# Dummy matmuls of a depthwise-separable kernel: operands from a built-in constant, loops unrolled, four passes on each side of dw

## The chip, the cores and the metric

The kernel runs on one core of one Trainium2 chip. The metric is device time in microseconds (us) of one execution.

## The reference

```python
B, H, W, C = x.shape            # 1, 384, 384, 384, bf16
k = dw.shape[0]                 # 1
for i in range(k):
    for j in range(k):
        out = out + xp[:, i:i+H, j:j+W, :] * dw[i, j][None, None, None, :]
return jnp.einsum('bhwc,cd->bhwd', out, pw)      # pw: 384 x 384
```

With k = 1 it is one matrix product in which the rows of pw are scaled by dw: 147,456 pixels by 384 channels, times a 384 x 384 matrix.

## The kernel before

The scaling by dw is folded into the weights, once, ahead of the main loop. A mask `eye` (GpSimd) is reduced to 0/1 selectors `sel` (VectorE), multiplied by dw to `sel_w`, and used in 18 small matmuls that write scaled and reordered rows of pw to PSUM (the "weight build"). Six evictions, five on ScalarE and one on VectorE, copy them to `w_r` (an eviction is a copy out of PSUM). The main loop then transposes x on VectorE, multiplies on TensorE (48 matmuls per tile, in 12 groups of four concurrent ones) and evicts on ScalarE.

While TensorE waits for its first data it runs dummy matmuls, meant to wake its clock (full rate came at 5.57 us in the profile before):

```python
def idle_work(n):
    with nc.tensor.Fori(0, n, 1) as _:
        for i in range(4):
            nc.tensor.matmul(PS[0][:, i, :D], lhsT=zero[32*i : 32*i+32, 0:P],
                             rhs=zero[32*i : 32*i+32, :], start=True, stop=True,
                             tile_position=(32*i, 0))

nc.tensor.wait_ge(s_zero, 1)
idle_work(3)
nc.tensor.wait_ge(s_seed, 2)
nc.tensor.wait_ge(s_dw, 16)
...                                  # three 1-row matmuls that turn dw into a column
idle_work(3)
nc.tensor.wait_ge(s_pw, 16)
times = {(1, 1): 3, (2, 0): 2}       # some groups of the weight build are repeated
...                                  # the weight build, k = 0, 1, 2
with nc.tensor.Fori(0, NS // 2, 1) as it:      # the main loop, 2 of 288 tiles a turn
    ...
```

One turn of the loop in `idle_work`, four matmuls side by side, is called a pass below. The loads at the start: dw and the first chunk of x on ScalarE's queue, pw and then the other chunks of x on SyncE's.

Of the kernel before, what the change touches and what calls it, by code (L numbers as in the profile page):

```python
# [7 lines left out]
BF16 = mybir.dt.bfloat16  # L8
F32 = mybir.dt.float32
U32 = mybir.dt.uint32  # L10
# [17 lines left out]
def kernel(  # L28
# [12 lines left out]
    nc = tc.nc  # L41
    P = nc.NUM_PARTITIONS
    B, H, W, C = x.shape
    assert dw.shape[0] == 1 and dw.shape[1] == 1, "only k=1 depthwise supported"
    D = pw.shape[1]
# [19 lines left out]
    consts = ctx.enter_context(tc.tile_pool(name="consts", bufs=1))  # L65
# [1 line left out]
    psum = ctx.enter_context(tc.tile_pool(name="psum", bufs=1, space=bass.MemoryType.PSUM))  # L67

    pw_n = consts.tile([P, 3, D], BF16, name="pw_n")
    ones = consts.tile([P, P], BF16, name="ones")  # L70
    eye = consts.tile([P, P], BF16, name="eye")
    sel = consts.tile([P, 2, 32], F32, name="sel")
    sel_w = consts.tile([P, 3, 2, 4, 32], BF16, name="sel_w")
    w_r = consts.tile([P, NB, 2, D], BF16, name="w_r")
    dw_row = consts.tile([1, C], BF16, name="dw_row")
    dw_f = consts.tile([P, 3], F32, name="dw_f")
    warm = consts.tile([P, 3], F32, name="warm")
    zero = consts.tile([P, D], BF16, name="zero")

    Xs = [bufp.tile([P, 4 * LMAX, C], BF16, name=f"X{i}") for i in range(NR)]  # L80
    Xl = bufp.tile([P, 4 * LONG, C], BF16, name="Xl")
# [2 lines left out]
    PS = [psum.tile([P, 4, 512], F32, name=f"ps{s}") for s in range(2)]  # L84
# [5 lines left out]
    s_a = [nc.alloc_semaphore(f"s_a{i}") for i in range(2)]  # L90
# [7 lines left out]
    s_sel = nc.alloc_semaphore("s_sel")  # L98
    s_w = nc.alloc_semaphore("s_w")
    s_wr = [nc.alloc_semaphore(f"s_wr{e}") for e in range(2)]  # L100
    s_seed = nc.alloc_semaphore("s_seed")
    s_zero = nc.alloc_semaphore("s_zero")

    with tc.tile_critical():  # L104
        def x_of(t):
# [60 lines left out]
        for o in range(NR):  # L166
            n = sum(n_parts[t] for t, c in enumerate(chunks) if c[0] % NR == o)
# [37 lines left out]


        def idle_work(n):
            with nc.tensor.Fori(0, n, 1) as _:
                for i in range(4):
                    nc.tensor.matmul(  # L210
                        PS[0][:, i, :D],
                        lhsT=zero[32 * i : 32 * i + 32, 0:P],
                        rhs=zero[32 * i : 32 * i + 32, :],
                        start=True,
                        stop=True,
                        tile_position=(32 * i, 0),
                    )

        nc.tensor.wait_ge(s_zero, 1)
        idle_work(3)  # L220

        nc.tensor.wait_ge(s_seed, 2)
        nc.tensor.wait_ge(s_dw, 16)
        for k in range(3):
            mm = nc.tensor.matmul(  # L225
                PS[1][:, 0, D + k : D + k + 1],
                lhsT=dw_row[:, P * k : P * k + P],
                rhs=ones[0:1, 0:1],
                start=True,
                stop=True,  # L230
            )
        mm.then_inc(s_df)
        idle_work(3)
        nc.tensor.wait_ge(s_pw, 16)
        times = {(1, 1): 3, (2, 0): 2}
        for k in range(3):
            nc.tensor.wait_ge(s_sw, k + 1)
            for r in range(2):
# [3 lines left out]
                for v in [0, 1] * times.get((k, r), 1):  # L242
                    mm = nc.tensor.matmul(  # L243
                        PS[(k + 1) % 2][:, 2 * r + v, :D],
                        lhsT=sel_w[64 * v : 64 * v + 64, k, r, :, :].rearrange("p q w -> p (q w)"),
                        rhs=pw_n[64 * v : 64 * v + 64, k, :],
# [5 lines left out]
        with nc.tensor.Fori(0, NS // 2, 1) as it:  # L252
# [2 lines left out]
                supertile(s, rv)  # L255


        nc.gpsimd.memset(warm[:], 0.0).then_inc(s_seed)
        nc.gpsimd.memset(zero[:].bitcast(U32), 0).then_inc(s_zero)  # L259
        nc.gpsimd.memset(ones[:], 1.0).then_inc(s_seed)  # L260
        nc.gpsimd.affine_select(  # L261
            out=eye[:],
            in_=ones[:],
            pattern=[[-1, P]],
            compare_op=mybir.AluOpType.is_equal,
            fill=0.0,
            base=0,
            channel_multiplier=1,
        )._wait_ge(s_seed, 2).then_inc(s_sel)
        for s in range(2):  # L270
            c = nc.scalar.copy(warm[:, s + 1 : s + 2], warm[:, 0:1])  # L271
            if s == 0:
                c._wait_ge(s_seed, 1)
            c.then_inc(s_a[s])

        def transposes(t, j):
            g, i, off, first, L = chunks[t]
# [18 lines left out]
        def w_out(i):  # L296
# [9 lines left out]
            in_=eye[:].rearrange("p (v w r) -> p r w v", v=2, r=2),  # L306
# [15 lines left out]
        for jj, (t, j) in enumerate(order):  # L322
            g, i, off, first, L = chunks[t]
            s = jj % 2
# [49 lines left out]
```

## Time and profile before

| | before |
|---|---|
| time, median of the first 3 runs | 575.13 us (575.04 to 575.19) |
| span of the profile | 573.3 us |
| TensorE busy | 566.7 us, 99% |
| VectorE / ScalarE busy | 507.4 / 419.0 us |
| first matmul of the main loop | 6.98 us |

Read it as three stretches: a start of 7 us, a main loop in which TensorE is never idle, and a tail of a few us that follows the last tile. The prediction shows the lines.

### The profile page before, as it was taken

To read this page: it belongs to the slowest core of one execution; us is meant where nothing else is said; L and a number is where in the kernel's file an instruction comes from. 1 tells how busy PE (TensorE), PEld (TensorE's weight loads), DVE (VectorE), ACT (ScalarE), POOL (GpSimd) and SP (SyncE) were. 2 spreads that over 40 slices of the span, in tenths; PEclk is the share of its full clock that TensorE was granted. 3 is DMA by queue.
4 is the path that set the end of the run, shared out by engine and by line. 5 is a ranking of instruction groups with operands and counts; after the bars stand their busy time and mean duration, and the time that the engine had idled before them with its cause. 6 is when DMAs were issued, how large, how long until landed. Compare 5 with 4: busy or idle time off the path is not lost.

```text
span 573.3 us, 29723 instructions
## 1 busy us (share of the span) xinstructions
PE 566.7 (99%) x13869; PEld 411.9 (72%) x13869; DVE 507.4 (89%) x584; ACT 419.0 (73%) x297; POOL 0.9 (0%) x8
## 2 busy tenths in 40 slices
PE   8999999999999999999999999999999999999996
PEld 5777777777777777777777777777777777777774
DVE  7898898898889889889888988988988898898895
ACT  6777777777777777777777777777777777777775
POOL 0000000000000000000000000000000000000000
PEclk9999999999999999999999999999999999999999
DMA  9999999999999999999999999999999999999676
GB/s 363 418 340 438 415 425 432 446 412 425 428 413 412 406 389 427 402 379 405 431 389 397 412 416 386 406 409 416 406 391 422 405 394 396 424 398 368 263 288 238
DMA packets 26453, 226.88 MB, mean 396 GB/s; under 512 B 1226, under 2 KB 6987, under 8 KB 22603
## 3 DMA queue, kind: packets, MB, share of 16 engines
q1 hardware_dynamic: 25264, 225.61, 97.1%
q10 hardware_dynamic: 1178, 1.18, 0.6%
q14 instruction: 10, 0.07, 0.0%
q8 instruction: 1, 0.02, 0.0%
HBM read 113.54 MB, written 113.25 MB: 396 GB/s over the span
## 4 chain that ended last, share of the span: by engine, by line
PE 97%; DMA 1%; ACT 1%; DVE 0%; issue 0%; SPq 0%
PE ps L193 97%; DMA pw_n<-in_pw_dram 1%; DMA out_dram<-O 0%; ACT w_r L299 0%; ACT O L336 0%; DVE O L334 0%; PE ps L243 0%; SPq L369 0%; SPq L104 0%
## 5 line engine op out<-in xcount | busy, mean ns | idle before, releaser
L193 PE MATMUL ps<-w_r,T 32*128 32x384 bf16 x13824 | 561.8, 321 | 0.5 <-ACT w_r L299 0.5
L286 DVE STREAM_TRANSPOSE T<-X 128x384 uint32<-128x384 uint32 x572 | 500.7, 877 | 55.4 <-DMA X<-in_x_dram 0.3
L336 ACT CAST O<-ps 128x1536 bf16<-128x1536 f32 x287 | 413.0, 1439 | 147.1 <-PE ps L193 147.1
L193 PEld LDWEIGHTS ps<-w_r,T 32*128 32x128 bf16 x13824 | 410.0, 93 | 152.3 <-issue 0.9
L299 ACT CAST w_r<-ps 128x768 bf16<-128x768 f32 x5 | 3.6, 819 | 1.1 <-PE ps L243 1.1
L210 PE MATMUL ps<-zero 32*128 32x384 bf16 x24 | 2.6, 494 | 1.4 <-POOL zero L259 1.4
L286 DVE STREAM_TRANSPOSE T<-Xl 128x384 uint32<-128x384 uint32 x4 | 3.5, 877 | 0.4
L334 DVE CAST O<-ps 128x384 bf16<-128x384 f32 x2 | 1.0, 553 | 3.1 <-DMA out_dram<-O 3.1
L271 ACT ACT_TABLE_LOAD x1 | 1.3, 1283 | 1.9 <-issue 1.9
L210 PEld LDWEIGHTS ps<-zero 32*128 32x128 bf16 x24 | 0.7, 99 | 2.6 <-issue 2.6
L243 PE MATMUL ps<-pw_n,sel_w 64*128 64x384 bf16 x18 | 2.3, 422 | 0.1
L243 PEld LDWEIGHTS ps<-pw_n,sel_w 64*128 64x128 bf16 x18 | 1.0, 121 | 1.4 <-issue 0.7
L304 DVE TENSOR_REDUCE sel<-eye 128x64 f32<-128x128 bf16 x1 | 0.3, 290 | 1.8 <-POOL eye L261 1.8
L299 DVE CAST w_r<-ps 128x768 bf16<-128x768 f32 x1 | 1.0, 958 | 1.0 <-PE ps L243 1.0
L333 ACT CAST O<-ps 128x384 bf16<-128x384 f32 x2 | 0.9, 482 | 0.5 <-PE ps L193 0.5
L314 DVE TENSOR_SCALAR sel_w<-sel,dw_f 128x256 bf16<-128x256 f32 x3 | 0.9, 347 | 0.0
L311 DVE COPY dw_f<-ps 128x3 f32<-128x3 f32 x1 | 0.2, 161 | 0.7 <-PE ps L225 0.7
L225 PEld LDWEIGHTS ps<-ones,dw_row 1*128 1x128 bf16 x3 | 0.2, 98 | 0.2 <-issue 0.2
L261 POOL TENSOR_SCALAR_AFFINE_SELECT eye<-ones 128x128 bf16<-128x128 bf16 x1 | 0.3, 294 | 0.1
L271 ACT COPY warm<-warm 128x1 f32<-128x1 f32 x2 | 0.3, 189 | 0.0
L259 POOL MEMSET zero<- 128x192 uint32 x1 | 0.3, 258 | 0.0
L225 PE MATMUL ps<-ones,dw_row 1*128 1x1 bf16 x3 | 0.2, 160 | 0.0
(6 smaller groups left out, 0.7 us busy)
## 6 DMA issues: line engine op xcount, KB each, us to landing
X<-in_x_dram SPq DMA_DIRECT2D x26, 3840.0 KB, 21.5
out_dram<-O SPq DMA_DIRECT2D x26, 3840.0 KB, 27.4
X<-in_x_dram SPq DMA_DIRECT2D x3, 1536.0 KB, 17.5
out_dram<-O SPq DMA_DIRECT2D x4, 768.0 KB, 9.3
out_dram<-O SPq DMA_DIRECT2D x2, 1536.0 KB, 14.6
X<-in_x_dram SPq DMA_DIRECT2D x3, 768.0 KB, 7.3
X<-in_x_dram SPq DMA_DIRECT2D x1, 2304.0 KB, 19.2
out_dram<-O SPq DMA_DIRECT2D x1, 2304.0 KB, 10.9
```

Of the source, the lines that this page charges most:

```text
L193: mm = nc.tensor.matmul(PS[s][:, q, :D], lhsT=Ts[s][32 * q : 32 * q + 32, b, par::2], rhs=w_r[32 * q : 32 * q + 32, b, par, :], start=(b, ...
L210: nc.tensor.matmul(PS[0][:, i, :D], lhsT=zero[32 * i : 32 * i + 32, 0:P], rhs=zero[32 * i : 32 * i + 32, :], start=True, stop=True, tile_p ...
L225: mm = nc.tensor.matmul(PS[1][:, 0, D + k : D + k + 1], lhsT=dw_row[:, P * k : P * k + P], rhs=ones[0:1, 0:1], start=True, stop=True,)
L243: mm = nc.tensor.matmul(PS[(k + 1) % 2][:, 2 * r + v, :D], lhsT=sel_w[64 * v : 64 * v + 64, k, r, :, :].rearrange("p q w -> p (q w)"), rhs ...
L259: nc.gpsimd.memset(zero[:].bitcast(U32), 0).then_inc(s_zero)
L271: c = nc.scalar.copy(warm[:, s + 1 : s + 2], warm[:, 0:1])
L286: ins = nc.vector.transpose(out=Tw[:, 3 * h : 3 * h + 3], in_=Xw[:, :, j, 96 * h : 96 * h + 96].rearrange("p k (b w) -> p b k w", w=32),)
L299: o = nc.vector.tensor_copy(out, in_) if e == 0 else nc.scalar.copy(out, in_)
L314: nc.vector.tensor_scalar_mul(sel_w[:, k], sel[:].unsqueeze(2).to_broadcast([P, 2, 4, 32]), dw_f[:, k : k + 1]).then_inc(s_sw)
L333: nc.scalar.copy(Ov[:, q, j, :], PS[s][:, q, :D]).then_inc(s_a[s])
L334: nc.vector.tensor_copy(Ov[:, q + 1, j, :], PS[s][:, q + 1, :D]).then_inc(s_d)
L336: a = nc.scalar.copy(Ov[:, :, j, :], PS[s][:, :, :D])
```

## The change

Its intent is to let the dummies begin as soon as the engines start, to make them denser (in the profile before they start 0.38 to 0.44 us apart where a loop turn lies between), and to save three memsets and TensorE's two waits for them. A constant 1.0 that the framework sets anyway, ahead of the opening barrier (at 0.37 us in the profile before), is read with a step of zero along the free dimension in place of two tiles filled for the purpose; the dummies so multiply ones, no longer zeros.

```diff
-    ones = consts.tile([P, P], BF16, name="ones")
-    zero = consts.tile([P, D], BF16, name="zero")
+    ones = nc.const_aps.tensor(1.0, [P, D], BF16)
...
         def idle_work(n):
-            with nc.tensor.Fori(0, n, 1) as _:
+            for _ in range(n):
                 for i in range(4):
                     nc.tensor.matmul(
-                        PS[0][:, i, :D],
-                        lhsT=zero[32 * i : 32 * i + 32, 0:P],
-                        rhs=zero[32 * i : 32 * i + 32, :],
+                        PS[0][:, 2 * (i % 2) + i // 2, :D],
+                        lhsT=ones[32 * i : 32 * i + 32, 0:P],
+                        rhs=ones[32 * i : 32 * i + 32, :],
...
-        nc.tensor.wait_ge(s_zero, 1)
-        idle_work(3)
-        nc.tensor.wait_ge(s_seed, 2)
+        idle_work(4)
         nc.tensor.wait_ge(s_dw, 16)
...
-        idle_work(3)
+        idle_work(4)
         nc.tensor.wait_ge(s_pw, 16)
...
-        nc.gpsimd.memset(warm[:], 0.0).then_inc(s_seed)
-        nc.gpsimd.memset(zero[:].bitcast(U32), 0).then_inc(s_zero)
-        nc.gpsimd.memset(ones[:], 1.0).then_inc(s_seed)
```

The mask `eye` and ScalarE's two seed copies read built-in constants too, and lose their waits (not printed here).

## The prediction

> **What bounds the kernel now.** The time is 575.13 us over three runs (575.04 to 575.19), the profiled span 573.3 us, so about 1.8 us lies outside the span; nothing in the diff touches that. I first read the page's shares of busy time and the chain that ended last, because the change touches only code that runs before the main loop.
>
> ```profile
> PE 566.7 (99%) x13869; PEld 411.9 (72%) x13869; DVE 507.4 (89%) x584; ACT 419.0 (73%) x297; POOL 0.9 (0%) x8
> L193 PE MATMUL ps<-w_r,T 32*128 32x384 bf16 x13824 | 561.8, 321 | 0.5 <-ACT w_r L299 0.5
> ```
>
> TensorE is busy 99% of the span; its main-loop matmuls lost 0.5 us to idling, once, before their first instruction. Then the chain in order of time:
>
> ```profile
> 1.02 3.02 DMA pw_n<-in_pw_dram
> 4.04 0.05 issue
> 4.09 0.52 PE ps L243 x2
> 4.61 0.02 issue
> 4.63 2.21 ACT w_r L299 x3
> 6.84 0.14 issue
> 6.98 557.90 PE ps L193 x13728
> 564.88 0.02 issue
> 564.90 1.45 ACT O L336
> ```
>
> So the start of the main loop at 6.98 is made of the load of pw (issued 1.02, landed 4.04), the first two weight-building matmuls (0.52), three evictions on ScalarE (2.21 together) and small hand-overs. From 6.98 on TensorE does not stop: 13,728 matmuls are 286 tiles of 48, and 557.90 / 286 = 1.951 us for each, or 162.6 ns for each of its 12 groups of four concurrent matmuls. Anything saved ahead of 6.98 comes off the time one for one, anything added comes on top, and nothing in the diff changes the loop. The timeline of the start shows where the changed instructions lie (columns: start, length, engine, line, operation, idle before it and its releaser):
>
> ```profile
> 1.05 0.26 POOL L259 MEMSET zero<- 128x192 uint32 x1
> 1.40 0.14 PEld L210 LDWEIGHTS ps<-zero 32*128 32x128 bf16 x4 [1.40 <-issue]
> 1.84 0.11 PEld L210 LDWEIGHTS ps<-zero 32*128 32x128 bf16 x4 [0.30 <-issue]
> 2.60 0.16 PEld L225 LDWEIGHTS ps<-ones,dw_row 1*128 1x128 bf16 x3 [0.22 <-issue]
> 3.51 0.11 PEld L210 LDWEIGHTS ps<-zero 32*128 32x128 bf16 x4 [0.27 <-issue]
> 4.08 0.13 PEld L243 LDWEIGHTS ps<-pw_n,sel_w 64*128 64x128 bf16 x4 [0.46 <-DMA pw_n<-in_pw_dram]
> 4.38 0.15 PEld L243 LDWEIGHTS ps<-pw_n,sel_w 64*128 64x128 bf16 x2 [0.17 <-issue]
> 4.70 0.15 PEld L243 LDWEIGHTS ps<-pw_n,sel_w 64*128 64x128 bf16 x2 [0.17 <-issue]
> 5.02 0.15 PEld L243 LDWEIGHTS ps<-pw_n,sel_w 64*128 64x128 bf16 x2 [0.17 <-issue]
> ```
>
> The reader is to see two things. The weight build at 4.08 waits for the DMA of pw, not for TensorE. And its groups start 0.32 us apart up to 5.34; the next three starts, in narrower views of the same timeline, are 5.62, 5.79 and 5.96, 0.17 us apart. The array runs at half rate until about 5.5 and at full rate after, so the dummy matmuls, which exist to wake the clock, have not done so by the time the weight build begins.
>
> [...] The trace [...] shows the switch about 4.1 us after the first dummy at 1.40. [...] the trace shows the passes that close a loop 0.38 to 0.44 us apart, against 0.32 of streaming, so a turn of the small loop costs some 0.06 to 0.12 us.
>
> **The change, part by part.**
>
> Memsets. Three go on GpSimd (warm, zero, ones: 0.10, 0.26 and 0.21 us). The built-in constant was already set at about 0.4 us in the kernel before, ahead of the opening barrier, so no new memset stands in. GpSimd has no part in the chain. The mask `eye`, written at 1.52 to 1.81, should start near 1.0; the reduction that reads it (1.84) moves up with it. Both have slack: the next DVE step waits for the dw matmuls, up to 2.88. On the path: 0.
>
> The wait of the first dummy. It started at 1.40 behind the 0.26 us memset. Without it TensorE starts when the barrier lets it go; the DMA issues and memsets of the others start at 0.98 to 1.02, so I take 1.0, which is 0.4 us earlier.
>
> Dummies ahead of dw. Before: three passes from 1.40, over by 2.60 (1.84 - 1.40 = 0.44; 0.43; 0.32). After: four passes without loop turns, 4 x 0.32 = 1.28, so 1.0 to about 2.3. The dw load is an unknown: it had landed by 2.60 but the trace does not say when. The dw matmuls start between 2.3 and 2.6, at most 0.3 us earlier. They lead to the DVE chain dw_f (0.16) and sel_w (0.34 each), which had its first product ready at 3.08 + 0.34 = 3.42, 0.6 us before pw landed. On the path: 0.
>
> Dummies behind dw. Before: three passes, last start 3.51, streaming to 3.83. After: four passes from 0.12 after the dw matmuls' start, 4 x 0.32 = 1.28: from 2.45 to 3.75 if dw comes at 2.33; from 2.75 to 4.03 if at 2.60. Either fits ahead of 4.04; the tail may cost up to 0.05 us in the later case. The total rises from 24 to 32 dummy matmuls.
>
> ScalarE's seed copies lose a wait, but they sat behind the table load (1.95 to 3.24), not behind the memset. On the path: 0. The constants read with a zero step and the changed order of PSUM banks concern dummies alone.
>
> The clock. This is the sole possible gain. If the array is warm by 4.09, the first pair of weight-building matmuls takes about 0.34 us in place of 0.50 (the warm matmuls of the loop last 321 ns, those at 4.09 are recorded with 0.50), about 0.16 us less, and the three evictions and the loop move up by it. TensorE being faster from 4.7 on gives nothing: ScalarE's evictions run back to back at 0.69 to 0.70 us each, and their inputs are ready early even at half rate (the third slice, started at 4.70, is done at 5.22; ScalarE takes it at 5.33). If the switch follows the first work by the same 4.1 us, it moves from 5.5 to 5.1: still too late for the pair at 4.09. [...] I give it one execution in three: 0.16 / 3 = 0.05 us on average. The sum is therefore 0 to -0.16, mean about -0.05, with +0.05 of risk behind dw.
>
> **The rivals.**
>
> The dummies warm the array in time for all of the weight build, and the kernel gains 0.16 us, perhaps a little more: about 574.95. For it: more work, begun earlier, without loop gaps. Against it: the present switch is 1.4 us too late, and only 0.4 us is gained.
>
> The fourth pass behind dw overruns the arrival of pw. For it: if dw lands late, the passes end at 4.03, and any extra cost of a pass (a zero-step read or weight load that streams slower, the 0.38 us of the looped passes) adds up: 4 x 0.38 = 1.52 from 2.75 is 4.27, 0.23 late. Against it: the 0.06 us over 0.32 is most simply the branch, which is gone. It would make 575.3.
>
> The start of the loop is delayed or held by something else that is near. The first DVE transposes run from 5.83 and end their first half by about 6.7, so a gain above 0.28 us would be cut there. The chain through the stores at the end follows the last matmuls and moves with them. A changed layout of SBUF or of the instruction stream that slows the loop: a 2% effect needs 11.5 us, 40 ns for each of 288 tiles; nothing in the views speaks for it.
>
> A late switch of the clock, after 6.98, would cost before and after alike; up to half of the time past 6.98. The three timings within 0.15 us speak against it having happened in any of them, and the earlier start makes it rarer still.
>
> **Range and chances.** Point: 575.13 - 0.05 = 575.08, rounded to 575.05 for the chance of a bit more. The sums span 574.95 to 575.35; the spread of three runs is 0.15, and a median taken at another time on perhaps another chip can sit a few tenths off. I take 574.5 to 575.6. A 2% step (11.5 us) is more than the whole start of 7 us, so a faster result beyond 2% is out of reach for any cause named here: 0.005; slower 0.005; within 2% 0.99.
>
> **What would show it.** In the changed kernel's timeline: the first dummy weight load near 1.0, dummy passes 0.32 us apart, `eye` near 1.0, the first weight-build load still at 4.0 to 4.1 released by the DMA of pw, the first eviction near 4.6, and the loop's first matmul at 6.8 to 7.0, then 1.951 us a tile. The warm step shows as groups 0.17 apart; if they are so from the start, the first eviction comes near 4.45. The prediction is wrong if the weight build starts later than 4.15 with TensorE as its releaser, if the load of pw lands at another time, or if the loop's time per tile changes.

## The result, and the profile after

The changed kernel took 575.10 us (median of 6 runs, 574.92 to 575.27); the kernel before, in those rounds, 575.12 us (575.04 to 575.7). The ratio is 0.9999, 95% interval 0.9986 to 1.0011: the same. A ratio here is the mean time of one kernel's fast runs over that of the other's of the same rounds, so not quite the ratio of the medians quoted.

The page's shares and groups, after:

```profile
PE 566.5 (99%) x13877; PEld 417.7 (73%) x13877; DVE 509.0 (89%) x584; ACT 418.7 (73%) x297; POOL 0.5 (0%) x5
L191 PE MATMUL ps<-w_r,T 32*128 32x384 bf16 x13824 | 561.8, 321 | 0.7 <-ACT w_r L289 0.7
```

Eight more dummy matmuls, three fewer GpSimd instructions, and the same 561.8 us of main loop. The chain that ended last, in order of time (start, length, what):

```profile
1.02 3.10 DMA pw_n<-in_pw_dram
4.12 0.05 issue
4.17 0.36 PE ps L239 x2
4.53 0.02 issue
4.55 2.21 ACT w_r L289 x3
6.76 0.14 issue
6.90 557.90 PE ps L191 x13728
```

It is the same chain as before. Two terms moved: pw landed at 4.12 in place of 4.04, and the first pair of the weight build took 0.36 us in place of 0.52, because the array (TensorE's multipliers) was at full rate by then: the groups from 4.17 to 4.83 start 0.16 to 0.17 us apart. The loop starts at 6.90 in place of 6.98, and lasts the same 557.90. The timeline of weight loads shows the rest (start, length, instruction, idle before it and its releaser):

```profile
1.11 0.14 PEld L208 LDWEIGHTS ps<-const-bfloat16-1.0 32*128 32x128 bf16 x8 [1.11 <-issue]
1.42 0.15 PEld L208 LDWEIGHTS ps<-const-bfloat16-1.0 32*128 32x128 bf16 x4 [0.17 <-issue]
1.74 0.15 PEld L208 LDWEIGHTS ps<-const-bfloat16-1.0 32*128 32x128 bf16 x4 [0.17 <-issue]
2.46 0.10 PEld L221 LDWEIGHTS ps<-const-bfloat16-1.0,dw_row 1*128 1x128 bf16 x1 [0.57 <-DMA dw_row<-in_dw_dram]
4.17 0.76 PEld L239 LDWEIGHTS ps<-pw_n,sel_w 64*128 64x128 bf16 x12 [0.86 <-DMA pw_n<-in_pw_dram]
```

The dummies start at 1.11 (before: 1.40), 0.32 us apart. dw, not TensorE, now holds the dw matmuls, up to 2.46; the weight build still waits for pw.

So is the 0.08 us a gain? That hangs on why the array was at full rate at 4.17. If denser dummies woke the clock by a fixed lag, every execution would have it. The experiments ask that.

### The profile page after: what moved, and what is told of

Its sections match the earlier page's. It is cut to its first block, busy times and chain, and to the rows that moved or that the text cites. A ratio compares the mean times of both kernels' runs of the same rounds, so it can differ in the third digit from the quotient of the medians.

```text
span 573.2 us, 29721 instructions
## 1 busy us (share of the span) xinstructions
PE 566.5 (99%) x13877; PEld 417.7 (73%) x13877; DVE 509.0 (89%) x584; ACT 418.7 (73%) x297; POOL 0.5 (0%) x5
## 4 chain that ended last, share of the span: by engine, by line
PE 97%; DMA 1%; ACT 1%; DVE 0%; issue 0%; SPq 0%
PE ps L191 97%; DMA pw_n<-in_pw_dram 1%; DMA out_dram<-O 0%; ACT w_r L289 0%; ACT O L326 0%; DVE O L324 0%; PE ps L239 0%; SPq L359 0%; SPq L102 0%
## 5 line engine op out<-in xcount | busy, mean ns | idle before, releaser
L191 PE MATMUL ps<-w_r,T 32*128 32x384 bf16 x13824 | 561.8, 321 | 0.7 <-ACT w_r L289 0.7
L191 PEld LDWEIGHTS ps<-w_r,T 32*128 32x128 bf16 x13824 | 415.9, 93 | 146.6 <-issue 1.0
L208 PE MATMUL ps<-const-bfloat16-1.0 32*128 32x384 bf16 x32 | 2.9, 515 | 1.1 <-SPq L102 1.1
```

The costliest lines, as they stand in the source:

```text
L191: mm = nc.tensor.matmul(PS[s][:, q, :D], lhsT=Ts[s][32 * q : 32 * q + 32, b, par::2], rhs=w_r[32 * q : 32 * q + 32, b, par, :], start=(b, ...
L208: nc.tensor.matmul(PS[0][:, 2 * (i % 2) + i // 2, :D], lhsT=ones[32 * i : 32 * i + 32, 0:P], rhs=ones[32 * i : 32 * i + 32, :], start=True ...
```

## The experiments

**My theory**: the time is the start of the main loop plus a constant, plus what the loop loses if the array is still at half rate when it begins; the start is pw's landing, the first pair, three evictions; the dummies act through the clock alone, and where the clock switches varies from execution to execution. **Rivals**: the denser dummies wake the clock by a fixed lag; or something else (transposes, the landing of x) holds the start anyway.

Each kernel ran five times, beside nine runs of the kernel before on the same chip; each also has one profile. All twelve kernels give right results.

**The kernel before, again.** No edit.

> The kernel before, unchanged, against itself: the floor of noise and a second look at its clock. All theories: ratio 1.000 within 0.0005, median 575.1 +- 0.15. If the clock's switch follows the first work by a fixed lag, the weight build's groups are again 0.32 us apart up to about 5.4 us and 0.17 after (switch about 4.1 us after the first dummy at 1.40). [...]

Measured: 575.28 us (574.99 to 575.31), ratio 0.9999, interval 0.9985 to 1.0012: that is the floor of noise. In its profile the weight build's groups are 0.32 us apart up to 5.66, so the switch is about 0.3 us later than in the first profile of the same program, and the third eviction has to wait for its input: the chain puts it at 6.14, and the loop starts at 7.09, not 6.98. The lag is not quite fixed, even here.

**The changed kernel, again.** No edit.

> The changed kernel again, a second look at its clock and five more times. [...] If the denser dummies wake the clock by a fixed lag, it is again before 4.17, the first pair takes 0.36 us and the loop starts within 0.1 us of 6.90. Either way the median is 575.1 +- 0.15; the slow tail of the kernel before (575.6 and 575.7 in 3 of 15 times) should be absent if the change lowers the chance of a late switch: highest below 575.5.

Measured: 575.02 us (574.82 to 575.85), ratio 1.0000 (0.9986 to 1.0013). Its timeline of weight loads:

```profile
4.09 0.13 PEld L239 LDWEIGHTS ps<-pw_n,sel_w 64*128 64x128 bf16 x4 [0.86 <-DMA pw_n<-in_pw_dram]
4.39 0.15 PEld L239 LDWEIGHTS ps<-pw_n,sel_w 64*128 64x128 bf16 x2 [0.17 <-issue]
4.71 0.15 PEld L239 LDWEIGHTS ps<-pw_n,sel_w 64*128 64x128 bf16 x2 [0.17 <-issue]
5.03 0.15 PEld L239 LDWEIGHTS ps<-pw_n,sel_w 64*128 64x128 bf16 x2 [0.17 <-issue]
5.35 0.72 PEld L239 LDWEIGHTS ps<-pw_n,sel_w 64*128 64x128 bf16 x8 [0.17 <-issue]
```

The same program as the profile after, and the groups are 0.32 us apart until about 5.6: the early switch is gone, the pair takes 0.52 again, the loop starts at 6.99. This fells the rival of a fixed lag. My own side-expectation fell as well: with 575.85 among its five times, the slow tail is not absent.

**No dummies.**

```diff
-        idle_work(4)
+        idle_work(0)
 ...
-        idle_work(4)
+        idle_work(0)
```

> The changed kernel with no dummy matmul at all. My theory (the start is the load of pw, the first pair, three evictions; dummies act through the clock alone): weight build at half rate (pair 0.52 us), first matmul of the loop near 6.95-7.05, and the loop's first 1 to 4 us at half rate, because TensorE's first dense work is at 4.1; 0.3 to 2 us over 575.1. Rival (the weight build alone wakes the clock in time, or dummies do nothing): within 0.2 us of 575.1.

Measured: 576.16 us (575.17 to 578.3; three of five at 576.2 to 576.3). The profile is that of the 578.3. Its chain:

```profile
1.54 5.58 DMA X<-in_x_dram
7.12 0.02 issue
7.14 0.87 DVE T L276
8.01 0.09 issue
8.10 560.08 PE ps L191 x13066
```

Two things came together: the first chunk of x landed at 7.12 (5.65 in the profile before, with the same loads), so the loop started at 8.10, not at the expected 6.95 to 7.05; and the loop's groups are 0.32 us apart up to 12.54. The interval of the ratio, 0.9998 to 1.0025, still touches 1, but the loop at half rate is seen directly. One execution without dummies took 575.17, as fast as any: dummies shift the odds (four of the five times here are 576.16 or more, none of eleven of the changed kernel is above 575.85), they are not needed each time.

**The constant with the old loops of three.**

```diff
-            for _ in range(n):
+            with nc.tensor.Fori(0, n, 1) as _:
 ...
-        idle_work(4)        # both places
+        idle_work(3)
```

> The changed kernel with the constant operands kept, but the dummies as in the kernel before: three passes in a loop on each side of dw. My theory: first dummy at 1.1, dw at about 2.46 (its load), weight build released by pw at 4.05-4.15, first pair 0.36 or 0.52 us by where the clock's switch falls, total 575.1 +- 0.15. Rival (the fourth pass and the unrolling are what woke the clock early): pair at 0.52 us, and 0.1 us more than the changed kernel.

Measured: 575.39 us (575.34 to 575.44). The chain:

```profile
1.02 3.01 DMA pw_n<-in_pw_dram
4.03 0.05 issue
4.07 3.06 PE ps L239 x18
7.13 0.03 issue
7.16 558.11 PE ps L191 x13728
```

Here the array stayed at half rate through the whole weight build, and then the build's own end, 7.13, sets the loop's start; the evictions were done before. The five times lie above my range, 0.3 us over the changed kernel, so this run speaks for the rival rather than for me; its interval, 0.9988 to 1.0016, holds 1. Five times within 0.1 us are odd for a switch that falls at random. The next run shows the same late clock, in one execution, without any loop.

**Three passes, unrolled.** `idle_work(3)` in both places of the changed kernel, nothing else.

> The changed kernel with three passes in place of four on each side, still unrolled and on the constant. [...] If the gaps of the loop decided there, it behaves like the changed kernel, 575.1.

Measured: 575.22 us (575.09 to 575.84), ratio 0.9998 (0.9985 to 1.0012). Its profile is of the 575.84: again a build at half rate throughout, a start at 7.18, and half rate up to 8.6 in the loop. Four other times of the same kernel are as fast as the kernel before. I had it late each time if the busy time of the dummies decides (at 0.32 us a pass, six are 1.92 us and eight 2.56), and like the changed kernel if the gaps of the loop do. Neither held: it is late once and on time four times. Whether the fourth pass changes the odds, five times can't tell; the count over all profiles, under the clock's own record below, says a little more.

**The unrolling alone, on the memset tile.** In the kernel before, `for _ in range(n)` and `idle_work(4)` twice.

> The kernel before with one part of the change alone: the dummies unrolled, four passes on each side of dw, still reading the tile that a memset fills. Sum of my theory: first dummy at 1.43, four passes 0.32 us apart to 2.71, dw there (its load has landed), four passes to 4.1, so the weight build may start 0 to 0.1 us after pw lands; loop start 6.85 to 7.1 by where the clock switches; median 575.1 +- 0.2. Rival (the constant, not the unrolling, woke the clock early): the switch stays after 5.3 us in this profile.

Measured: 575.22 us (574.9 to 575.86), ratio 1.0001 (0.9987 to 1.0014). The switch is at about 5.5, the pair takes 0.52, the loop starts at 7.00: the other half of the change alone does nothing to be seen either. That the switch stays after 5.3 is what the rival said, but the changed kernel's second profile has it there too, so it decides nothing. The chain in this profile runs through x (landed 6.01) and the first transpose, so this third way to the start is level with the evictions.

**Eight passes behind dw.** `idle_work(8)` in the second place.

> The changed kernel with eight passes behind dw in place of four, an overrun on purpose. My theory (all before the loop's first matmul counts one for one): the passes end 0.3 us late (if half of them are warm, 0.17 us each) to 0.9 us late (all cold, 0.32 us each); the weight build is released by TensorE itself near 4.5-5.0, and the time is 575.4 to 576.0. Rival (a wait near by, such as the transposes or the evictions, already sets the start, so TensorE has slack there): within 0.15 us of 575.1.

Measured: 576.07 us (575.28 to 576.15), ratio 1.0008 (0.9994 to 1.0022). The chain of its profile (of 576.12):

```profile
2.69 2.58 PE ps L208 x29
5.28 0.45 PE ps L239 x2
5.73 0.02 issue
5.75 2.21 ACT w_r L289 x3
7.96 0.14 issue
8.10 557.90 PE ps L191 x13728
```

Now TensorE's dummies, not pw, release the weight build; the loop starts 1.12 us later than before and the span is 1.13 us longer, both a little beyond the 0.9 us I allowed. So there is no slack ahead of the loop beyond the wait for pw. The two executions at 575.28 and 575.51 would fit an array that switched early, so that the eight passes took less; they have no profile.

**pw in two parts.**

```diff
-        nc.sync.dma_start(pw_n[:], ...).then_inc(s_pw, 16)
+        nc.sync.dma_start(pw_n[:, 0, :], pw[0:P, :]).then_inc(s_pw0, 16)
+        nc.sync.dma_start(pw_n[:, 1:3, :], ...).then_inc(s_pw, 16)
 ...
-        idle_work(4)
-        nc.tensor.wait_ge(s_pw, 16)
+        idle_work(2)
+        nc.tensor.wait_ge(s_pw0, 16)       # and s_pw ahead of k = 1
```

> The changed kernel with pw loaded in two parts, the first third by itself with its own semaphore, and two passes behind dw in place of four so that TensorE is free for it. My theory (the landing of pw starts the chain): first third lands near 3.3-3.7, loop start moves up to about 6.6, where the transposes of the first chunk stop it; 574.8, or 0.3 us less than the changed kernel. Rival (the start is set by the transposes or the clock anyway): no gain, 575.1; if fewer dummies leave the clock cold through the loop's start, 575.3 to 576.

Measured: 577.38 us (575.76 to 577.68), ratio 1.0027 (1.0013 to 1.0041): a miss. The first part landed at 3.14, but the chain shows the second:

```profile
1.46 4.37 DMA pw_n<-in_pw_dram
5.83 0.05 issue
5.88 2.42 PE ps L243 x10
8.29 0.03 issue
8.32 559.21 PE ps L193 x13728
```

It landed only at 5.83, and TensorE, idle in between, was at half rate up to 11.1. The first x, issued at 1.55 on the other queue, is the suspect. The packets fit: between 3.5 and 4.5 us the queue that holds pw moved 65 packets, 0.05 MB, and that of x 90, 0.27 MB. In the kernel before, pw's queue had moved 0.29 MB by 3.5, so pw was all but through before most of x came.

**First x behind pw.** `load_x(0)` on SyncE behind pw, in place of ScalarE's queue; pw in one piece, four passes.

> The changed kernel with the first load of x moved from ScalarE's queue to SyncE's, behind pw, so that it can't compete with pw. My theory (pw's landing starts the chain, and what landed the second part of pw late in the split run was the competition of x): pw lands at or before 4.05, the first chunk of x before 5.6; the loop starts at 6.75 to 7.0 with the clock as it falls; 575.0 +- 0.2. Rival (order of issue does not matter to landings): landings as in the changed kernel, x near 5.6-6.0 or later, 575.1.

Measured: 575.14 us (574.98 to 575.32), ratio 0.9997 (0.9983 to 1.0010). The first x landed at 4.97 (5.65 before), pw at 4.01 (4.04). So an unsplit pw, issued first, lost next to nothing to x; and with a build at half rate throughout (its end at 7.09; the loop starts at 7.14, beyond my range) nothing came of the earlier x.

**Both: pw in two parts, first x behind them.** Two passes behind dw.

> The split of pw once more (first third by itself, two passes behind dw), now with the first x behind both parts in SyncE's queue. My theory: first part at about 3.1, second before 4.3, the first eviction at 4.2 and all three evictions back to back, loop start near 6.55 where the clock is warm by 6.5: 574.8 at best; where the clock switches late the loop starts cold and the time is 575.3 to 576.5. Rival (the second part is late whatever is in the other queue): second part after 5 us again, 577.

Measured: 574.67 us (574.55 to 575.19), against 575.2 (574.96 to 575.94) of the kernel before in the same rounds; ratio 0.9991, interval 0.9977 to 1.0004. The chain:

```profile
2.63 0.66 PE ps L210 x4
3.29 0.07 issue
3.36 3.08 PE ps L243 x18
6.44 0.03 issue
6.47 558.07 PE ps L193 x13127
```

The two parts landed at 3.12 and 3.97, so it was x in the other queue that had held the second: 4.37 us from issue to landing beside x, 2.5 with x behind. That is one profile each, but the times bear it out: four of five were 576.66 or more there, and here none is above 575.19. The chain also shows that the two passes behind dw, over at 3.29, now hold the build for 0.2 us after the first part has landed. The loop starts at 6.47, half a microsecond earlier, and the median follows by half a microsecond. Four of the five times lie below the lowest of the nine of the kernel before. It is the best kernel here, by 0.09%; the stated interval just reaches 1.

**The same with three passes behind dw.** `idle_work(3)` in the second place.

> As the run before it, with three passes behind dw in place of two: a little more work for the clock, the first pair at most 0.1 us later. If dummies act through the clock alone: median no higher than with two passes, fewest times above 575.6. If only the start of the chain counts: 0.1 us slower than with two.

Measured: 575.00 us (574.88 to 575.38), ratio 0.9995 (0.9982 to 1.0009). It reads 0.3 us slower than with two, and the chain shows x.

```profile
1.93 3.86 DMA X<-in_x_dram
5.79 0.02 issue
5.82 0.88 DVE T L280
6.69 0.09 issue
6.78 558.08 PE ps L193 x13728
```

x landed at 5.79 here and at 5.42 in the run before, with the same loads in the same order. The third pass had its part too: the build started at 3.55 in place of 3.36 and ended near 6.60 in place of 6.44, so without the late x it alone would have cost some 0.2 us of the 0.31. Once pw no longer holds the start, the dummies or the first x do.

**No repeats in the weight build.** `times = {}`.

> The changed kernel without the repeated matmuls inside the weight build (6 groups in place of 9). In the profiles where the array stayed at half rate through the whole build, the build's own end (7.09 to 7.13 us) set the loop's start, not the three evictions. If that reading is right, without the repeats the evictions set the start whatever the clock does: 6.9 to 7.0 even when the build is at half rate throughout. With less work the clock may switch later, which then costs inside the loop: median 575.0 to 575.6. If the reading is wrong (something else holds the start in those profiles), a cold build again gives a start near 7.15.

Measured: 575.09 us (575.03 to 576.6), ratio 1.0006 (0.9993 to 1.0020). In its profile the last two matmuls of the build still take 0.49 us together, as at half rate (a pair at full rate took 0.36):

```profile
6.01 0.49 PE L239 MATMUL ps<-pw_n,sel_w 64*128 64x384 bf16 x2
```

So the case in question, half rate to the end of the build, did occur, and the three evictions set the start, 7.02 (the chain goes from 4.67 through 2.21 us of evictions). With the repeats such a build set it itself, at 7.14 to 7.18. My reading holds: against these profiles, the repeats cost 0.12 to 0.16 us of the start when the clock is late. One time of 576.6 suggests that less work can be dear; it has no profile.

**All of them in one sum.** If the theory holds, the span of each profile follows from two numbers: when the loop starts, and how much longer than 0.1625 us (the mean distance of two groups of the loop in the profiles before and after) the loop's first groups are apart. Both are read from the starts of the matmuls in the trace. The sum is relative to the profile before (start 6.98, no slow group).

| profile | loop starts | slow in the loop until | start shift + loss in the loop | span, less 573.27 |
|---|---|---|---|---|
| after | 6.90 | none | -0.08 | -0.08 |
| before, again | 7.09 | none | +0.11 | +0.12 |
| after, again | 6.99 | none | +0.01 | +0.02 |
| no dummies | 8.10 | 12.54 | 1.13 + 2.16 = 3.29 | +3.30 |
| constant, old loops | 7.16 | 7.69 | 0.18 + 0.20 = 0.38 | +0.40 |
| eight behind | 8.10 | none | +1.12 | +1.13 |
| unrolled alone | 7.00 | none | +0.02 | +0.03 |
| pw in two | 8.32 | 11.10 | 1.35 + 1.31 = 2.66 | +2.66 |
| three unrolled | 7.18 | 8.63 | 0.20 + 0.64 = 0.84 | +0.85 |
| x behind pw | 7.14 | none | +0.16 | +0.17 |
| both | 6.47 | 6.95 | -0.51 + 0.16 = -0.35 | -0.34 |
| both, three passes | 6.78 | 7.28 | -0.20 + 0.18 = -0.02 | -0.02 |
| no repeats | 7.02 | none | +0.04 | +0.05 |

Worked example, no dummies: 14 group distances from 8.10 to 12.54 are 4.43 us; 14 x 0.1625 = 2.27; the loss is 2.16. All thirteen sums are within 0.02 us of the spans, so in these executions nothing behind the loop's first groups moved the time. The sum says where time went; why a loop started when it did is in the chains.

**The clock's own record.** Each trace also holds the granted clock as the chip recorded it (the array `0/clock` of trace.npz; no view prints it). It puts the switch to full rate at 5.57 us in the profile before and at 3.91 after, and in the two repeats at 5.88 and 5.61; in none of the four does it disagree with the spacing of the groups. So one and the same program switches at different times. Counted from the first dummy, the switch came after 2.8 us (after), 4.2 (before) and 4.5 (both repeats). With the old loops on the constant, whose dummies began at 1.17, the loop's groups were slow until 7.69, 6.5 us later, though the weight build had run unbroken from 4.07 to 7.13.

How much work a switch takes these runs don't show. What can be counted is this: of the eight profiles with fewer than eight passes none was at full rate before 5 us, of the six with eight or more one was, the profile after. So the fourth pass may matter to the early switch, as the rival in the run with the old loops said, but if so, seldom.

## Why the prediction was right

- **What bounds the kernel**, the start chain plus a loop without slack: right, shown by the table, and by the overrun of eight passes, which cost 1.12 us at the start and 1.13 in the span.
- **Memsets, seed copies, first wait: 0 on the path.** Right: first dummy at 1.11 (I took 1.0), `eye` at 1.10, and the weight build still released by pw.
- **dw the unknown, between 2.3 and 2.6.** It released TensorE at 2.46; the last pass behind it started at 3.42 to 3.48, well ahead of pw. The rival of an overrun did not happen; the zero-step operands stream at 0.32 us a pass, the distance of the weight build's groups at half rate too.
- **The clock, worth 0.16 us if warm by 4.09.** The size was exact (0.52 to 0.36). I gave it one execution in three, a guess; of the profiles with four passes on each side that start at 1.11 or 1.12 and have pw in one piece (after, after again, x behind pw, no repeats), one in four shows it, too few for a rate. That the profile after caught it was luck.
- **"TensorE being faster from 4.7 on gives nothing"** was too simple. It holds for a switch at 5.5. With a switch at about 5.9 the third eviction waits (start 7.09), and with half rate to the end the build itself sets the start, 7.14 to 7.18. I had checked only the third slice. ScalarE's third eviction reads the fourth one, whose repeated matmuls ended at 5.95 in the profile before, close to the 6.02 at which ScalarE took it, and at 6.10 in the repeat.
- **"A late switch": "the three timings within 0.15 us speak against it".** This was too easy, without hurting the total. Of 47 times of the kernel before, 6 are 575.6 to 575.94, and of 11 of the changed kernel one is 575.85. That these are late switches is argued from the profiles of 575.84 and 578.3, which are; the slow times of these two kernels have no profile, and a late first x (7.12 us in the profile of 578.3) would do as well. "Rarer still" is not shown by the times: 6 in 47 and 1 in 11 are the same within chance. The changed kernel's own two profiles, of other executions, show the switch at 3.91 and 5.61, so what made its 575.85 is open. The profiles point the prediction's way: of the six with eight or more passes none has slow groups in the loop, of the eight with fewer six have.
- **Sums.** Passes from 2.45 end at 3.73, not 3.75; nothing hangs on it.
- **The number.** 575.05 predicted, 575.10 measured. Taking all runs together, the medians are 575.17 (47 times) and 575.08 (11 times): 0.09 us apart, where one kernel's times spread over 1 us. So a gain of the predicted 0.05 us is neither shown nor excluded.

What stays open: what sets the time of the clock's switch (five times within 0.1 us in the run with the old loops do not look like chance), what the slow times without a profile are, and whether the changed order of PSUM banks in the dummies, or ones in place of zeros, does anything; neither was run alone.

## What to carry to other kernels

Find what the last wait ahead of the main loop waits for before making the filler better: here a load of 288 KB ended at 3.93 to 4.12 us whatever the dummies did, and the only run with a lower median than the changed kernel's by more than 0.1 us was one that moved loads. Count in how many profiles the filler has brought full rate early: here, before 5 us, in none of eight with fewer than eight passes and in one of six with eight or more. Check an early-clock gain in a second profile of the same program, because the switch can fall elsewhere (at 3.91 and 5.61 us here). And when a load at the start is split, look at what another queue loads at the same time: the same split cost 2 us (half of it through the clock) or gained 0.5 us by where the first load of x stood.
